# Cluster assignment of the later head pairs: centroids held still while the tokens move

## The chip, the cores and the metric

The kernel runs on one core of one Trainium2 chip. The metric is the device time of one execution in microseconds (us). Five engines work side by side, each through its own list of instructions in order: TensorE (PE; its weight loads are listed apart as PEld), VectorE (DVE), ScalarE (ACT), GpSimd (POOL) and SyncE (SP), which here issues the DMAs.

## The reference, cut to what matters

Attention in which a query sees only the keys of its own cluster, and two wide layers behind it:

```python
# q, k, v: (2, 8, 768, 64); centroids: (8, 16, 64)
q_assign = np.argmax(np.einsum('bhsd,hcd->bhsc', q_n, c_n), axis=-1)   # rows normalised
k_assign = np.argmax(np.einsum('bhsd,hcd->bhsc', k_n, c_n), axis=-1)
mask = q_assign[:, :, :, None] == k_assign[:, :, None, :]
scores = np.where(mask, scale * np.matmul(q, k.transpose(0, 1, 3, 2)), -1e9)
attn = softmax(scores);  x = np.matmul(attn, v)      # -> (1536, 512)
h = x @ w_in;  x = (h * np.cos(h)) @ w_out           # 512 -> 2048 -> 512
h = x @ w2_in; x = elu(h) @ w2_out
```

The change is in the two `einsum` products with the 16 centroids of each head.

## The kernel before

There are 16 heads (2 batches of 8), taken in 8 pairs of 768 tokens, that is 6 blocks of 128. Each head and block of queries is a step, 96 steps in all, 12 to a pair. A step multiplies q with k (`qk`), takes the row maximum on DVE, the exponential on ACT (`P`), turns P on TensorE (`turn`, 6 transposes), and splits what was turned into a high part on ACT (`p_hi`, tile PH) and a low part on DVE (`p_lo`, tile PL), so that TensorE's products with v (`av`, tile px) keep the precision. All fp32 products of the kernel are made of such pairs, hi and lo.

Beside the 12 steps of one pair stands the preparation of the next. `raw_pe` turns k and q on TensorE (tile pt_raw), `raw_out` and `raw_copy` bring them to SBUF on ACT, `raw_low` makes the low part on POOL (one of the four on DVE), and `stack` issues 6 DMAs for each of k and q that lay hi and lo of one head above each other in tiles X0, X1 (and hi alone in T0, T1). `sims_pe` multiplies each of the 24 blocks of a pair (k and q, 2 heads, 6 blocks): the block of the stack is the stationary operand, and the 32 columns of `CC` (16 centroids high, 16 low) move. `sims_add` on DVE adds the high and the low half (2 instructions a pair). Then `sims_scale`, `sims_max`, `sims_eq`, `sims_first`, `best` and `assign` find the cluster, `mask_pe` turns it, `mask_out` writes it, and DMAs lay it under the T tiles, where the next pair's `qk` reads it. The first pair has its own code, one head at a time (`first_pe` and so on), and keeps `sims_pe`.

Seven PSUM buffers matter here: two for the scores of `qk` (tile s), so that `qk` of a step waits for the exponential of two steps before; one for px; and three (`pt_tile`), taken in turn by `turn`, `raw_pe`, the similarities and the mask.

The order on each engine is written by hand in tables: `FIRST`, `PAIR`, `STEP`, `HALF`, `UNIT`, `LAST`, `MLP`, `WINO`, `WB` give each part a time in units of a step, the parts are sorted by it and recorded in that order, and each engine works through its own share in order. `OWN` and tables like `RAW_ON` say on which engine a part runs. After step 96 come the two wide layers (lines 222, 281 and 481 are their products).

Of the kernel before, what the change touches and what calls it, by code (L numbers as in the profile page):

```python
# [61 lines left out]
SSQ = 'quarter'  # L62
XOUT = {0: 'pool', 1: 'pool'}
# [1252 lines left out]
```

## Time and profile before

| | |
|---|---|
| time, median of 3 runs | 780.28 us (776.9 to 780.54) |
| the profiled execution's own time | 778.07 us |
| its span from first to last instruction | 776.3 us |
| PE, DVE, ACT, POOL busy in the span | 98%, 81%, 71%, 50% |
| PE's granted clock | 1.00 |
| head, until the first `qk` (line 1034) starts | 18.61 us |
| attention, until the last `turn` (line 1057) ends | 264.07 us |
| both wide layers and the output | the rest |

The profiled execution is 2.2 us under the median of the three and 1.2 us over the fastest. Busy time is the union of what an engine's records cover; the matmul records overlap each other (one of 128x384 has 340 to 370 ns, and the next starts after about 177), so the pace of PE is read from the chain of work, in which each instruction counts from the end of the one before. The chain names, at every moment, the work that the end of the program waited for. Line numbers are those of the kernel before.

### The profile page before, as it was taken

Reading aid. Unit: us, or ns where it says so; the run is one execution under the profiler, and the core shown is the slowest. Engines: PE = TensorE matmul, PEld = TensorE weight load, DVE = VectorE, ACT = ScalarE, POOL = GpSimd, SP = SyncE. Lnnn points to the kernel's source line nnn. Section 1 sums busy time; section 2 is a strip of 40 time slices with the busy share of each in tenths; the row PEclk is TensorE's granted clock in tenths of the full one; section 3 lists DMA queues with packets and bytes.
Section 4 is the critical chain, followed back from the end, with each engine's and each line's share of the span. In section 5 each row is a group of like instructions: output and inputs, shape, how many; then the busy total and the mean of one; then the engine's idle time right before and its main releaser. Section 6 shows DMA issues by size and latency. Waiting matters only on the chain.

```text
span 776.3 us, 13062 instructions
## 1 busy us (share of the span) xinstructions
PE 761.6 (98%) x4579; PEld 682.2 (88%) x4579; DVE 631.8 (81%) x1026; ACT 548.0 (71%) x1030; POOL 387.0 (50%) x453
## 2 busy tenths in 40 slices
PE   6999999999999999999999999999999999999998
PEld 5899999999898888888999999988888999999996
DVE  7989899899899999997999844699997687754442
ACT  5898998988989978867666755668645554554343
POOL 5676676766866634354555522205236456632221
PEclk9999999999999999999999999999999999999999
DMA  4646647648447295011113168564001222233221
GB/s 104 143 115 148 159 102 163 142 91 197 109 105 264 44 379 194 1 42 73 70 62 123 55 231 291 198 225 155 1 1 41 95 82 82 82 104 115 82 82 54
DMA packets 72145, 93.27 MB, mean 120 GB/s; under 512 B 31440, under 2 KB 52432, under 8 KB 72080
## 3 DMA queue, kind: packets, MB, share of 16 engines
q1 hardware_dynamic: 72080, 92.44, 39.7%
q8 instruction: 36, 0.59, 0.3%
q14 instruction: 29, 0.24, 0.1%
HBM read 58.75 MB, written 15.78 MB: 96 GB/s over the span
## 4 chain that ended last, share of the span: by engine, by line
PE 86%; DVE 6%; ACT 4%; DMA 2%; issue 1%; SPq 0%; POOL 0%; ACTq 0%; DVEq 0%
PE a L281 32%; PE h L481 20%; PE h L222 11%; PE pt L1057 6%; PE px L1088 6%; PE s L1034 3%; PE s L1037 3%; PE pt_sim L869 2%; DVE m L1042 2%; DVE PL L1077 1%; DMA X1k<-lo 1%; PE pt_raw L728 1%; ACT PH L1071 1%; DMA X1q<-lo 1%; ACT P L1048 1%
## 5 line engine op out<-in xcount | busy, mean ns | idle before, releaser
L545 POOL TENSOR_TENSOR GL<-A,GH 128x512 fp32r<-128x512 f32 x60 | 81.1, 1357 | 150.5 <-ACT GH L94 118.6
L281 PE MATMUL a<-GH,slot 128*128 128x512 f32 x384 | 122.9, 390 | 0.0
L281 PE MATMUL a<-slot,GH 128*128 128x512 f32 x384 | 118.5, 389 | 0.0
L1077 DVE TENSOR_TENSOR PL<-pt,PH 128x384 fp32r<-128x384 f32 x192 | 98.3, 548 | 18.1 <-ACT PH L1071 16.9
L1071 ACT ACTIVATE PH<-pt 128x384 fp32r<-128x384 f32 x192 | 84.3, 495 | 15.3 <-PE pt L1057 15.1
L1042 DVE TENSOR_REDUCE m<-s 128x1 f32<-128x768 f32 x96 | 90.8, 946 | 2.1 <-PE s L1037 1.9
L1048 ACT ACTIVATE P<-s,m 128x768 f32<-128x768 f32 x96 | 87.1, 907 | 0.3
L281 PEld LDWEIGHTS a<-GH,slot 128*128 128x128 f32 x384 | 72.2, 188 | 14.6
L1057 PE MATMUL pt<-ident,P 128*128 128x128 f32 x576 | 83.0, 277 | 0.7 <-DVE PL L1077 0.7
L222 PE MATMUL h<-XH,slot 128*128 128x512 f32 x256 | 83.0, 390 | 0.0
L281 PEld LDWEIGHTS a<-slot,GH 128*128 128x128 f32 x384 | 70.9, 188 | 13.7
L481 PE MATMUL h<-XH,slot 128*128 128x256 f32 x384 | 79.2, 281 | 0.0
L281 PE MATMUL a<-GL,slot 128*128 128x512 f32 x192 | 75.0, 390 | 0.0
L281 PE MATMUL a<-slot,GL 128*128 128x512 f32 x192 | 74.7, 389 | 0.0
L1057 PEld LDWEIGHTS pt<-ident,P 128*128 128x128 f32 x576 | 66.6, 140 | 7.4 <-DVE PL L1077 2.2
L392 POOL TENSOR_TENSOR X<-slot 128x512 f32<-128x512 f32 x32 | 50.1, 1578 | 39.8 <-DVE sums L435 34.9
L481 PEld LDWEIGHTS h<-XH,slot 128*128 128x128 f32 x384 | 63.9, 189 | 0.1
L503 DVE TENSOR_TENSOR X<-X 128x256 f32<-128x256 f32 x32 | 24.7, 772 | 46.8 <-ACT X L501 46.8
L94 ACT ACTIVATE GH<-A 128x512 fp32r<-128x512 f32 x85 | 53.2, 625 | 10.1 <-DVE A L253 4.3
L501 ACT ACTIVATE X<-h 128x512 f32<-128x512 f32 x32 | 19.1, 597 | 54.2 <-PE h L481 54.0
L222 PEld LDWEIGHTS h<-XH,slot 128*128 128x128 f32 x256 | 48.0, 188 | 10.0
L1088 PE MATMUL px<-PL,V 128*128 128x384 f32 x192 | 56.2, 368 | 0.0
(198 smaller groups left out, 2007.0 us busy)
## 6 DMA issues: line engine op xcount, KB each, us to landing
raw<-in_moe_w_in_dram SPq DMA_DIRECT2D x32, 512.0 KB, 6.4
raw<-in_moe_w_out_dram SPq DMA_DIRECT2D x32, 512.0 KB, 7.3
sd<-sums SPq DMA_DIRECT2D x32, 384.0 KB, 2.3
sums<-sd SPq DMA_DIRECT2D x32, 384.0 KB, 3.5
nat_k<-in_k_dram SPq DMA_DIRECT2D x16, 192.0 KB, 4.8
nat_q<-in_q_dram SPq DMA_DIRECT2D x16, 192.0 KB, 4.7
nat_v<-in_v_dram SPq DMA_DIRECT2D x8, 384.0 KB, 4.9
xr<-row SPq DMA_DIRECT2D x32, 96.0 KB, 3.6
```

The source lines that it names most:

```text
L94: nc.scalar.activation(out=out, in_=in_, func=AF.Copy)
L222: nc.tensor.matmul(h, lhsT=a[:, kd, :], rhs=b, start=(kd == 0 and i == 0), stop=(kd == NKD - 1 and i == 2))
L281: nc.tensor.matmul(accs[m, t][e], lhsT=a, rhs=b, start=(f == 0 and i == 0), stop=(f == NF - 1 and i == 2))
L392: eng.tensor_tensor(out=u[:, i].rearrange("p e n -> p (e n)").rearrange("p (k f) -> p k f", k=NKD), in0=f32(ih), in1=f32(il), op=ALU.add)
L481: nc.tensor.matmul(o, lhsT=x[:, k], rhs=piece(y, k), start=(k == 0 and n == 0), stop=(k == 1 and n == 2))
L545: eng.tensor_tensor(out=GL, in0=A, in1=f32(GH), op=ALU.subtract)
L1042: nc.vector.tensor_reduce(out=m, in_=st[n]["s"][:, :, 0:HW], axis=AX.XY, op=ALU.max, negate=True)
L1048: nc.scalar.activation(out=P, in_=st[n]["s"][:, :, 0:HW], func=AF.Exp, bias=st[n]["m"], accum_out=den_all[:, u % NDEN, j, r, 0:1])
L1057: nc.tensor.transpose(pt[:, c * 128:(c + 1) * 128], st[n]["P"][:, e, c * 128:(c + 1) * 128], ident)
L1071: nc.scalar.activation(out=ph, in_=pt, func=AF.Copy)
L1077: nc.vector.tensor_tensor(out=pl, in0=pt, in1=f32(ph), op=ALU.subtract)
L1088: nc.tensor.matmul(tx[g][:, 0:HW], lhsT=V2s[pp][:, j, c, :], rhs=halves[g][a][:, c, :], start=(n == 0), stop=(n == 2 * C - 1))
```

## The change

For pairs 2 to 8, `sims_pe` and `sims_add` are replaced by four parts for each half (384 tokens) of the pair.

`pair_cen` (once, on POOL) lays the centroids of each pair on a block diagonal: tile `CCD` has 128 rows (64 dimensions of head 0, 64 of head 1) and, of its 128 columns, those of the wanted tensor filled. `pair_sims` holds CCD still and moves 384 tokens of `hi` and `lo` of q and of k, 4 matmuls that add up in one PSUM tile: k's into 64 rows, q's into 128. It reads `hi` and `lo` themselves, not the stacks that the DMAs make. `pair_keep` copies the result to SBUF (ACT, `KEEP_ON`), `pair_back` turns it back with 3 transposes, and `pair_add` (DVE) adds the high and the low columns. What follows works on the same numbers in another layout. All order tables are remade, `HI2_ON` moves one copy of the first pair from POOL to ACT, and 41 of the 152 entries of `OWN` change engine.

```diff
-PAIR = {'raw_pe:k:0': -2.1142, 'raw_out:k:0': -1.1899, 'raw_low:k:0': 0.3012, ...
+PAIR = {'raw_pe:k:0': -1.2162, 'raw_out:k:0': -1.1229, 'raw_low:k:0': 2.1627, ...
...
+KEEP_ON = {0: "act", 1: "act"}
...
-HI2_ON = {('k', 0): 'act', ('k', 1): 'pool', ('q', 0): 'act', ('q', 1): 'act'}
+HI2_ON = {('k', 0): 'act', ('k', 1): 'act', ('q', 0): 'act', ('q', 1): 'act'}
...
+        CCD = pre.tile([128, NP, 8 * NCL], F32R, name="CCD")
+        turned, backs = {}, {}
+        def pair_cen():
+            need(("cc",))
+            nc.gpsimd.memset(f32(CCD), 0.0)
+            c4 = CC.rearrange("p (a j) n -> p a j n", j=2)
+            for j in range(2):
+                rows = slice(64 * j, 64 * j + 64)
+                copy_on("pool", CCD[rows, :, (4 + 2 * j) * NCL:(6 + 2 * j) * NCL], f32(c4[rows, :, j]))
+            made("ccd")
+        def pair_sims(pp, e):
+            need(("ccd",), *[(x, pp, w, e) for x in ("hi", "lo") for w in "kq"])
+            pt = turned[pp, e] = pt_tile("pt_sim")
+            for w, i in (("q", 0), ("k", 0), ("k", 1), ("q", 1)):
+                n = 128 if w == "q" else 64
+                nc.tensor.matmul(pt[0:n, 0:HW], lhsT=CCD[:, pp % NP, 128 - n:128], rhs=hls[w][i][:, half_slice(e)],
+                                 start=(w == "q" and i == 0), stop=(w == "q" and i == 1))
+            made("pair_sims", pp, e)
+        def pair_keep(pp, e):
+            need(("pair_sims", pp, e))
+            pt = turned[pp, e]
+            turned[pp, e] = pre.tile([128, HW], F32, tag="turned", bufs=2, name="turned")
+            copy_on(KEEP_ON[e], turned[pp, e], pt[:, 0:HW])
+            made("pair_keep", pp, e)
+        def pair_back(pp, e):
+            need(("pair_keep", pp, e))
+            pt = backs[pp, e] = pt_tile("pt_back")
+            for c in range(C // 2):
+                cs = slice(c * 128, (c + 1) * 128)
+                nc.tensor.transpose(pt[:, cs], turned[pp, e][:, cs], ident)
+            made("pair_back", pp, e)
+        def pair_add(pp, e):
+            need(("pair_back", pp, e))
...
+            nc.vector.tensor_reduce(
+                out=sims[pp][:, e * HC:(e + 1) * HC].rearrange("p c b n -> p (c b) n"),
+                in_=backs[pp, e][:, 0:HW].rearrange("p (b t n) -> p b n t", t=2, n=NCL), axis=AX.X, op=ALU.add)
+            made("pair_add", pp, e)
```

TensorE's list in the preparation of the fifth pair, before: half of k's similarities, single ones between the steps' work (L1057 `turn`, L1088 `av`, L1034 and L1037 `qk`); q's 12 stand in one stretch three steps on.

```order
L1088 MATMUL px<-PH,V_1164 128x384 x2
L1057 MATMUL pt<-ident,P 128x128 x3
L869 MATMUL pt_sim<-CC,X0k 128x32
L1057 MATMUL pt<-ident,P 128x128 x3
L1088 MATMUL px<-PL,V_1164 128x384 x3
L869 MATMUL pt_sim<-CC,X1k 128x32
L869 MATMUL pt_sim<-CC,X0k 128x32
L869 MATMUL pt_sim<-CC,X1k 128x32
L1034 MATMUL s<-X0k,X0q 128x384 x2
```

The same place in the changed kernel (L893 `pair_sims`, L909 `pair_back`, L1106 `turn`, L1137 `av`, L1083 and L1086 `qk`), from the second half's `pair_sims` on.

```order
L893 MATMUL pt_sim<-hi,CCD 128x384
L893 MATMUL pt_sim<-hi,CCD 64x384
L893 MATMUL pt_sim<-lo,CCD 64x384
L893 MATMUL pt_sim<-lo,CCD 128x384
L1083 MATMUL s<-X0k,X0q 128x384 x2
L1086 MATMUL s<-T0k,T0q 128x384 x2
L1106 MATMUL pt<-ident,P 128x128 x3
L909 MATMUL pt_back<-ident,turned 128x128 x3
L1106 MATMUL pt<-ident,P 128x128 x3
L1137 MATMUL px<-PH,V_1649 128x384 x3
L1137 MATMUL px<-PL,V_1649 128x384 x3
L909 MATMUL pt_back<-ident,turned 128x128 x3
```

24 matmuls that move 32 columns are gone; 8 that move 384 and 6 transposes stand in fewer places, and one `qk` and three transposes stand between a `pair_sims` and the `pair_back` that waits for its copy.

ScalarE's list at the same place, before (L1048 exponential, L1071 PH, L1130 and L1141 what leaves px, L737 and L743 hi and raw):

```order
L743 ACTIVATE raw<-pt_raw 128x384
L737 ACTIVATE hi<-pt_raw 128x384
L1048 ACTIVATE P,den<-s,m 128x768
L1071 ACTIVATE PH<-pt 128x3x128 x2
L1048 ACTIVATE P,den<-s,m 128x768
L1071 ACTIVATE PH<-pt 128x3x128 x2
L1130 ACTIVATE xr<-px 64x384
L1141 ACTIVATE X<-px 64x384
L1048 ACTIVATE P,den<-s,m 128x768
```

And in the changed kernel (L95 is `pair_keep`; L738, L744, L1097, L1120, L1179, L1190 are the six lines above):

```order
L738 ACTIVATE hi<-pt_raw 128x384
L744 ACTIVATE raw<-pt_raw 128x384
L1097 ACTIVATE P,den<-s,m 128x768
L1120 ACTIVATE PH<-pt 128x3x128 x2
L1097 ACTIVATE P,den<-s,m 128x768
L95 ACTIVATE turned<-pt_sim 128x384
L1120 ACTIVATE PH<-pt 128x3x128 x2
L1179 ACTIVATE xr<-px 64x384
L95 ACTIVATE turned<-pt_sim 128x384
L1190 ACTIVATE X<-px 64x384
L1097 ACTIVATE P,den<-s,m 128x768
```

The two copies stand between two exponentials, where none stood.

## Rows read from the trace of the kernel before

**Rows 1.** The page: busy time by engine, and the chain's shares by engine.
```profile
PE 761.6 (98%) x4579; PEld 682.2 (88%) x4579; DVE 631.8 (81%) x1026; ACT 548.0 (71%) x1030; POOL 387.0 (50%) x453
...
PE 86%; DVE 6%; ACT 4%; DMA 2%; issue 1%; SPq 0%; POOL 0%; ACTq 0%; DVEq 0%
```

**Rows 2.** Windows: length, busy us by engine, clock, DMA; pairs, transition, wide layer.
```profile
96.37:126.63 30.26, 30.23 (x213) 28.32 (x212) 27.50 (x55) 27.88 (x65) 21.34 (x33) 1.00 0.60 137
126.63:157.57 30.94, 30.43 (x214) 28.36 (x212) 28.19 (x56) 28.02 (x65) 21.32 (x33) 1.00 0.65 142
...
187.82:218.67 30.85, 30.27 (x213) 28.29 (x212) 27.64 (x55) 27.99 (x65) 21.33 (x33) 1.00 0.61 144
...
226.00:258.00 32.00, 30.45 (x200) 28.51 (x199) 30.26 (x56) 31.59 (x69) 21.96 (x20) 1.00 0.55 183
...
300.00:350.00 50.00, 50.00 (x245) 42.35 (x244) 47.79 (x67) 36.99 (x56) 21.69 (x17) 1.00 0.06 25
```

**Rows 3.** Chain of waits in time order, 113 to 128 us: start, us, what.
```profile
113.44 0.53 PE px L1088 x3
...
114.30 0.35 PE s L1034 x2
...
116.68 0.33 PE pt_raw L728 x3
...
118.70 0.81 PE pt L1057 x6
...
119.86 0.45 PE s L1034 x2
...
123.29 0.66 PE pt L1057 x6
...
126.63 1.14 PE pt_sim L869 x11
```

**Rows 4.** Timeline of PE: similarities that waited for a DMA; in brackets idle, releaser.
```profile
27.35 0.36 PE L869 MATMUL pt_sim<-CC,X1k 128*128 128x32 f32 x2 [0.54 <-DMA X1k<-lo]
...
156.92 0.25 PE L869 MATMUL pt_sim<-CC,X1q 128*128 128x32 f32 x1 [0.43 <-DMA X1q<-lo]
...
210.43 0.37 PE L869 MATMUL pt_sim<-CC,X1k 128*128 128x32 f32 x2 [0.51 <-DMA X1k<-lo]
```

**Rows 5.** Groups of instructions: busy us, mean ns, then idle before.
```profile
L743 ACT ACTIVATE raw<-pt_raw 128x384 f32<-128x384 f32 x21 | 10.4, 496 | 0.2
...
L876 DVE TENSOR_REDUCE sm<-pt_sim 128x192 f32<-128x384 f32 x14 | 7.7, 552 | 0.1
```

**Rows 6.** Timeline of ACT in the same pair.
```profile
104.64 0.86 ACT L1071 ACTIVATE PH<-pt 128x384 fp32r<-128x384 f32 x2
105.38 0.92 ACT L1048 ACTIVATE P<-s,m 128x768 f32<-128x768 f32 x1
...
118.42 0.94 ACT L1048 ACTIVATE P<-s,m 128x768 f32<-128x768 f32 x1
119.21 0.25 ACT L1048 ACTIVATION_READ_ACCUMULATOR P<-s,m 128x1 f32 x1
...
121.36 0.91 ACT L1071 ACTIVATE PH<-pt 128x384 fp32r<-128x384 f32 x2 [0.26 <-PE pt L1057]
```

**Rows 7.** Timeline of POOL: the last low part of the same pair.
```profile
118.65 1.00 POOL L752 TENSOR_TENSOR lo<-raw,hi 128x384 fp32r<-128x384 f32 x1 [0.42 <-ACT hi L737]
```

**Rows 8.** Chain of waits in the head.
```profile
16.81 0.36 DVE sm L876
17.17 0.28 DVE M L935
...
17.50 0.52 PE pt_mask L944 x3
```

**Rows 9.** Timeline of POOL in the head: first square and low part of pair 2.
```profile
18.02 1.47 POOL L828 TENSOR_TENSOR sq<-nat_k 128x768 f32<-128x768 f32 x1 [0.22 <-issue]
...
21.23 1.00 POOL L752 TENSOR_TENSOR lo<-raw,hi 128x384 fp32r<-128x384 f32 x1
```

More of the change, by code (lines that the diff above doesn't have):

```diff
@@ new lines @@
+PAIR = {'raw_pe:k:0': -1.2162, 'raw_out:k:0': -1.1229, 'raw_low:k:0': 2.1627, 'raw_pe:k:1': -0.5582, 'raw_out:k:1': -0.3666, 'raw_low:k:1': 0.0171, 'stack:k': 3.2351, 'raw_pe:q:0': 1.144, 'raw_out:q:0': 1.3604, 'raw_low:q:0': 2.2027, 'raw_pe:q:1': 1.644, 'raw_out:q:1': 2.0896, 'raw_low:q:1': 2.6137, 'stack:q': 3.2967, 'square:k': -0.448, 'square:q': -1.0107, 'sum_sq:k': 1.6306, 'sum_sq:q': 1.1242, 'seed': 2.2387, 'norms': 4.9678, 'sims_scale': 6.3541, 'sims_max': 6.3759, 'sims_first': 6.6512, 'load_nat:k': -7.1463, 'load_nat:q': -7.2335, 'load_nat:v': 3.0434, 'raw_copy:k:0': -0.8153, 'raw_copy:k:1': -0.0355, 'raw_copy:q:0': 1.2556, 'raw_copy:q:1': 2.276, 'best': 7.3105, 'sims_eq': 6.5858, 'values_hi:0': 7.8287, 'values_lo:0': 7.9611, 'values_hi:1': 8.019, 'values_lo:1': 9.0409, 'norm_step:0': 2.8631, 'norm_step:1': 3.0606, 'norm_step:2': 3.4295, 'norm_step:3': 3.6274, 'assign': 7.8532, 'mask_pe': 8.4304, 'mask_out': 8.6084, 'pair_sims:0': 3.9595, 'pair_sims:1': 3.043, 'pair_keep:0': 4.3053, 'pair_keep:1': 3.5714, 'pair_back:0': 4.5395, 'pair_back:1': 5.207, 'pair_add:0': 4.8399, 'pair_add:1': 5.6206}
@@ L871, in sims_pe @@
                 made("sim", pp, w, n)
+        CCD = pre.tile([128, NP, 8 * NCL], F32R, name="CCD")
[31 more added lines that the diff above has]
+            need(("pair_back", pp, e))
+            if pp not in sims:
+                sims[pp] = pre.tile([128, C, 4, NCL], F32, tag="sm", bufs=1, name="sm")
+            nc.vector.tensor_reduce(
+                out=sims[pp][:, e * HC:(e + 1) * HC].rearrange("p c b n -> p (c b) n"),
+                in_=backs[pp, e][:, 0:HW].rearrange("p (b t n) -> p b n t", t=2, n=NCL), axis=AX.X, op=ALU.add)
+            made("pair_add", pp, e)
         def sims_add(pp, w, js):
@@ L882, in sims_of @@
         def sims_of(pp, js):
-            return sims[pp][:, :, js[0]] if len(js) == 1 else sims[pp].rearrange("p w h c n -> p w (h c) n")
+            return sims[pp][:, :, js[0]] if len(js) == 1 else sims[pp]
         def sims_scale(pp, js):
-            need(("norm", (pp, js)), ("sims", pp, "k", js), ("sims", pp, "q", js))
+            need(("norm", (pp, js)), *([("pair_add", pp, e) for e in range(2)] if pp else [("sims", pp, w, js) for w in "kq"]))
             sm = sims_of(pp, js)
+            r = nrm[pp].rearrange("p w h c -> p c (w h)") if pp else of_heads(nrm[pp], js)
             eng = nc.vector if pp == 0 else nc.gpsimd
-            eng.tensor_tensor(out=sm, in0=sm, in1=of_heads(nrm[pp], js).unsqueeze(3).to_broadcast(list(sm.shape)),
+            eng.tensor_tensor(out=sm, in0=sm, in1=r.unsqueeze(3).to_broadcast(list(sm.shape)),
                               op=ALU.mult)
@@ L919, in best @@
             if pp not in bests:
-                bests[pp] = pre.tile([128, 2, 2, C], F32, tag="best", bufs=1, name="best")
-            nc.vector.tensor_reduce(out=of_heads(bests[pp], js), in_=sims_of(pp, js), axis=AX.X, op=ALU.max)
+                bests[pp] = pre.tile([128, C, 4] if pp else [128, 2, 2, C], F32, tag="best", bufs=1, name="best")
+            nc.vector.tensor_reduce(out=bests[pp] if pp else of_heads(bests[pp], js), in_=sims_of(pp, js), axis=AX.X, op=ALU.max)
             made("best", pp, js)
@@ L931, in assign @@
             else:
-                sh = [128, 4, C, NCL]
-                m = M.rearrange("p c b n -> p b c n")[:, :, :, 0:NCL]
-                be = bests[pp].rearrange("p w h c -> p (w h) c")
+                sh = [128, C, 4, NCL]
+                m = M[:, :, :, 0:NCL]
+                be = bests[pp]
             nc.vector.tensor_tensor(out=m, in0=desc.unsqueeze(1).unsqueeze(1).to_broadcast(sh),
@@ L1213 @@
                         at(t0, fn, pp, *own)
-                elif fn in (raw_pe, raw_out, raw_copy, raw_low, stack, values_hi, values_lo):
+                elif fn in (raw_pe, raw_out, raw_copy, raw_low, stack, values_hi, values_lo, pair_sims, pair_keep, pair_back,
+                            pair_add):
                     at(t0, fn, pp, *own)
```

21 lines of the change are left out of this document (10 added, 11 removed).

## The prediction

> **What bounds the kernel now.** I read the page first, then windows of busy time over single pairs, then the chain of waits inside one pair, and last the timelines of ScalarE and GpSimd there. The page gives TensorE 98% and puts 86% of the chain on it [rows 1]. Busy time alone proves little, since matmul records overlap. In a clean pair of 30.26 us TensorE has 30.23, ScalarE 27.88, VectorE 27.50 and GpSimd 21.34 us [rows 2]; the chain of that pair runs through TensorE's instructions one behind the other at a steady pace, six transposes in 0.66 us, three products with 384 moving columns in 0.53, eleven similarities in 1.14 [rows 3]. So there the pace of TensorE is the time, and work taken from it is time saved, as long as ScalarE, which idles only 30.26 - 27.88 = 2.38 us a pair, keeps up. Two of the pairs are longer by 0.68 and 0.59 us [rows 2], each holding a similarity that waited for a DMA of the stacks, and a third such wait of 0.54 us stands in the head [rows 4]. Between 226 and 258 us ScalarE is full instead (31.59 of 32.00) [rows 2]. In the wide layers TensorE has 50.00 of 50.00 us, so nothing is to be had there.
>
> **What goes from TensorE, per pair (7 pairs).** 24 similarities at 1.14 / 11 = 0.104 us are 2.49. They also delay what follows: the scores behind a run of them take 0.45 for two matmuls in place of 0.35, three times in this pair, and the six transposes behind four of them 0.81 in place of 0.66 [rows 3]: 0.45 more. Together 2.94 us.
>
> **What comes to it.** 8 products with 384 moving columns at 0.53 / 3 = 0.177 are 1.41; 6 transposes at 0.33 / 3 = 0.110 (as the raw ones) are 0.66 [rows 3]; 2.07 together. Gain 0.87 a pair, 6.1 us in seven. The trace shows no product with this block diagonal, so I bound it: at the dearest rows, 0.45 / 2 = 0.225 and 0.81 / 6 = 0.135, the new work is 2.61, and with no delays credited to the old the pair loses 0.12; at the cheapest, 0.35 / 2, it gains 0.88. I take 0.87, since the products of px have the same shape in stationary and moving operand. 7 pairs: +0.8 to -6.2, taken -6.1.
>
> The 32 columns that a similarity moves do not explain 0.104 us, which the row shows. [...]
>
> **What comes to the others.** ScalarE gets 2 copies of 128x384 a pair, 496 ns each as the copy `raw` [rows 5], 0.99 of busy time; where it works without a break the next starts 0.37 us later (two PH start at 104.64 and what follows them at 105.38, half of 0.74 each [rows 6]), so 0.74 of its pace. VectorE's two sums keep their input, 128x384, and their 552 ns [rows 5]: nothing. GpSimd gets a memset and two small copies once.
>
> **The new waits.** The scores of a step wait for the exponential of two steps before (two buffers). In this pair ScalarE has no idle from 104.64 to 121.36 us, through the whole raw stage [rows 6]. At its end an exponential ends at 119.21 + 0.25 = 119.46, and TensorE's next scores start at 119.86 [rows 3]: 0.40 us to spare. The two copies stand just there, ahead of the next exponential, and push it by 0.74: a wait of 0.34. Behind the waiting scores TensorE holds the transposes and the products with v, so this is paid in full. The wait of `pair_sims` itself seems covered: the last low part ends at 119.65 [rows 7], 2.64 us after its raw transposes (117.01 [rows 3]), and in the new order TensorE has 6 products, a step's scores, 6 transposes and 3 products between, 1.06 + 0.70 + 0.66 + 0.53 = 2.95. If that cover is gone, low parts cost what they are late. `pair_back` has scores and three transposes (1.03) to cover a copy of 0.50. I count 0.35 a pair, 2.5 us; the bounds are 0 (ScalarE's 2.38 us take it up) and 0.99 a pair, 6.9.
>
> **The DMA waits.** `pair_sims` reads hi and lo, so the stacks are needed only by the next pair's scores, some steps later. 0.68 + 0.59 + 0.54 = 1.8 us go [rows 2, 4]; at least 1.0, if a low part is late where the DMA was.
>
> **The head.** The first mask waits for an `assign` that stands behind a sum of the last similarities (0.36, at 16.81) though it does not need it [rows 8]. In the new order it stands ahead of that sum: -0.4. Against it, GpSimd now has both squares of the second pair ahead of the three low parts: one square with its sums takes 21.23 - 18.02 = 3.2 us [rows 9], so the low parts end near 18.0 + 6.4 + 3.0 = 27.4, where the old similarities began at 27.35 [rows 4]. I leave that at nothing; bounds -1 and +1 for the head.
>
> **The rest.** From 226 to 258 us ScalarE's work stays as it is, so 0; bounds -1.5 and +1.5 (TensorE's 32.00 - 30.45) [rows 2]. In the wide layers the remade order can only lose: +0.5, one gap such as those of rows 4; bounds 0 and +3.
>
> **The sum.** -6.1 + 2.5 - 1.8 - 0.4 + 0 + 0.5 = -5.3 against the profiled execution's 778.07, so 772.8. That execution is 2.2 us under the median of the three and 1.2 over the fastest; the mean of the four is 778.95, 0.9 higher. On that level the forecast is 773.6.
>
> **Rivals.**
>
> *ScalarE takes back what TensorE gives.* If the copies cost their whole 0.99 a pair at the place above, the pair changes by 0.99 - 0.87 = +0.12. With the DMA waits gone the sum is 0.8 - 1.8 - 0.4 + 0.5 = -0.9: 778.0. For it: ScalarE's long stretch without idle. Against it: 2.38 us of idle in the same pair, and shorter use of the three PSUM buffers (the old similarities of k hold one from 2.2 to 4.3 in `PAIR`, about two steps).
>
> *Slower: ScalarE becomes the bound of every pair.* The place is the raw stage. If TensorE already follows ScalarE there, through the two score buffers, then what it saves is worth nothing and each pair grows by the copies, 7 x 0.99 = 6.9; `pair_sims` then waits for hi and lo that ScalarE brings later, so the DMA waits are only exchanged. 6.9 - 0.4 + 0.5 = +7.0: 786. It decides from the point where the copies exceed the idle that ScalarE can reach in order: 0.99 against the 0.40 us above, if the 2.38 us lie elsewhere for good. Against it: the chain of the pair is TensorE's alone [rows 3]. The Trainium skill's page Trainium Kernel Development and Optimization (section "Best Practices") speaks for this side: tiling speeds up compute "but not PSUM evacuation", and the change buys TensorE's time with two more evacuations; no run here shows yet which of the two ends last.
>
> *More gained.* No new wait, and the transition gains 1.0: -5.3 - 2.5 - 1.0 = -8.8, 770.1.
>
> **How the numbers follow.** Forecast 0.55 (its own range 770 to 777), ScalarE takes it back 0.23, slower 0.13, more gained 0.09. The range 769.5 to 781 leaves out the slower case and a little below. A measurement of this kernel can tell about 0.5% from no change, 3.9 us, so faster means under 776.4 and slower over 784.2: faster holds the forecast but for its upper end, the case of more gained and a little of the second, 0.57; slower 0.13; between 0.30.
>
> **What would show it.** Clean pairs of 29.5 to 30.0 us in the windows, TensorE still full in them; no wait of TensorE for a DMA between 20 and 220 us; scores (L1034's successor) waiting for an exponential, some 0.3 us a pair; ScalarE at 28.9 us a pair. Pairs of 30.3 and longer with ScalarE without idle would make the forecast wrong, as would gaps of TensorE in the wide layers of more than 1 us, or `pair_sims` waiting for GpSimd in each pair.

## The result, and the profile after

The changed kernel takes 783.85 us (median of 7 runs, 782.89 to 784.69) where the kernel before takes 780.03 (7 runs, 776.9 to 781.38): ratio 1.0058, 95% interval 1.0038 to 1.0078. It is slower by 0.6%, and the time lies 10 us above the forecast of 773.6 and 2.8 above the upper end of the range. The profiled execution took 784.19, with a span of 782.3 (776.3 before). Lines 52 to 872 have moved by 1 (L222 is now L223), those from 890 to 1213 by 49 (L1034 is L1083).

Four points that both traces show, by the start of the same instruction, split the 6.0 us between the two spans (the medians are 3.8 apart):

| | before | after | change |
|---|---|---|---|
| raw transposes of q (pt_raw), third pair | 53.22 | 54.03 | head +0.81 |
| the same, eighth pair | 205.25 | 204.91 | five periods 152.03, 150.88: -1.15 |
| first product of the next token block, h<-XH (L481, L482) | 342.87 | 347.82 | stretch 137.62, 142.91: +5.29 |
| end of the span | 776.3 | 782.3 | 433.4, 434.5: +1.05 |

The head's part is known only to about 1 us: four other traces below with the same code up to there (e1, e3, e5, e11) pass the first point at 53.71, 53.66, 54.58 and 54.61, so it lies between +0.4 and +1.4.

The page after (busy by engine, then the chain's shares by engine), and windows of one pair, of two stretches behind attention and of the wide layer (columns as in [rows 2]):

```profile
PE 760.7 (97%) x4509; PEld 678.2 (87%) x4509; DVE 613.6 (78%) x1030; ACT 559.2 (71%) x1051; POOL 379.9 (49%) x445
...
PE 68%; DVE 10%; DMA 8%; ACT 8%; SPq 2%; issue 2%; POOL 1%; ACTq 0%; POOLq 0%
```
```profile
117.33:147.51 30.18, 29.47 (x202) 27.68 (x201) 27.05 (x53) 28.90 (x67) 21.37 (x34) 1.00 0.61 130
...
280.00:285.00 5.00, 2.10 (x8) 1.38 (x7) 5.00 (x6) 5.00 (x8) 0.00 (x0) 0.93 1.07 374
285.00:290.00 5.00, 5.00 (x18) 3.98 (x17) 3.15 (x5) 2.66 (x4) 0.00 (x0) 0.73 1.06 376
300.00:350.00 50.00, 50.00 (x231) 41.78 (x230) 44.63 (x58) 40.04 (x62) 21.93 (x14) 1.00 0.04 17
```

A pair lasts 30.18 us, 0.08 less than the clean one of [rows 2], with TensorE 29.47 busy instead of 30.23 and ScalarE 28.90 instead of 27.88. TensorE stands still for 2.90 of the 5 us from 280, and in the 5 us behind them the granted clock is 0.73. What TensorE waited for (total, times, longest):

```profile
PE pt L1106 <- ACT hi L738: 3.3, 6, 0.6
PE h L223 <- DVE A L254: 2.9, 1, 2.9
PE pt L1106 <- DVE PL L1126: 2.6, 9, 0.8
...
PE h L482 <- DVE sums L363: 0.8, 1, 0.8
```

The first is six times the same place, one in each of six pairs; TensorE and ScalarE there (start, duration, then in brackets the idle time and who ended it):

```profile
115.06 0.52 PE L1086 MATMUL s<-T0k,T0q 80*128 80x384 f32 x2
116.13 0.88 PE L1106 MATMUL pt<-ident,P 128*128 128x128 f32 x6 [0.55 <-ACT hi L738]
```
```profile
113.78 0.89 ACT L1120 ACTIVATE PH<-pt 128x384 fp32r<-128x384 f32 x2
114.69 0.48 ACT L1179 ACTIVATE xr<-px 64x384 f32<-64x384 f32 x1
115.20 0.49 ACT L744 ACTIVATE raw<-pt_raw 128x384 f32<-128x384 f32 x1
115.59 0.48 ACT L738 ACTIVATE hi<-pt_raw 128x384 fp32r<-128x384 f32 x1
```

`turn` needs a PSUM buffer that pt_raw holds until `hi` has read it, and `hi` stands behind xr and raw on ScalarE. The new work itself, in the same pair:

```profile
120.12 0.51 PE L893 MATMUL pt_sim<-hi,CCD 128*128 128x384 f32 x2
120.47 0.52 PE L893 MATMUL pt_sim<-lo,CCD 128*64 128x384 f32 x2
...
124.46 0.49 PE L909 MATMUL pt_back<-ident,turned 128*128 128x128 f32 x3
```

Two products in 0.35, as forecast (0.177 each). Behind attention, TensorE and VectorE:

```profile
280.26 0.39 PE L282 MATMUL a<-GH,slot 128*128 128x512 f32 x1
283.54 0.50 PE L223 MATMUL h<-XH,slot 128*128 128x512 f32 x1 [2.90 <-DVE A L254]
...
285.23 1.05 PE L223 MATMUL h<-XH,slot 128*128 128x512 f32 x2
...
287.75 0.62 PE L223 MATMUL h<-XH,slot 128*128 128x512 f32 x2
```
```profile
281.07 1.22 DVE L177 TENSOR_TENSOR slot<-u,slot 128x1024 fp32r<-128x1024 f32 x1
282.20 1.28 DVE L254 TENSOR_TENSOR A<-h,R 128x512 f32<-128x512 f32 x2
```

The second A ends at 283.48, and the first product of the fifth F block (a slice of 128 of the 2048 hidden columns) starts at 283.54. From 285.23 to 286.51 three products take 1.28 us, from 287.75 to 288.43 three take 0.68: 3 x 512 columns are 1.28 us at 1.2 GHz and 0.64 at 2.4, the two levels of TensorE's clock.

### The profile page after: what moved, and what is told of

It is laid out like the page before. It is cut to its first block, busy times and chain, and to the rows that moved or that the text cites. A ratio compares the mean times of both kernels' runs of the same rounds, so it can differ in the third digit from the quotient of the medians.

```text
span 782.3 us, 12962 instructions
## 1 busy us (share of the span) xinstructions
PE 760.7 (97%) x4509; PEld 678.2 (87%) x4509; DVE 613.6 (78%) x1030; ACT 559.2 (71%) x1051; POOL 379.9 (49%) x445
## 4 chain that ended last, share of the span: by engine, by line
PE 68%; DVE 10%; DMA 8%; ACT 8%; SPq 2%; issue 2%; POOL 1%; ACTq 0%; POOLq 0%
PE a L282 32%; PE h L482 20%; PE h L223 11%; DMA row<-sum 4%; DVE m L1091 3%; DVE PL L1126 3%; ACT PH L1120 2%; DMA xr<-row 2%; ACT P L1097 2%; PE pt L1106 2%; PE px L1137 2%; DMA nat_q<-in_q_dram 1%; PE pt_sim L893 1%; ACT Z L1016 1%; SPq L609 1%
## 5 line engine op out<-in xcount | busy, mean ns | idle before, releaser
L546 POOL TENSOR_TENSOR GL<-A,GH 128x512 fp32r<-128x512 f32 x60 | 83.8, 1401 | 144.6 <-ACT GH L95 109.4
L1126 DVE TENSOR_TENSOR PL<-pt,PH 128x384 fp32r<-128x384 f32 x192 | 101.0, 547 | 12.7 <-ACT PH L1120 11.0
L1106 PE MATMUL pt<-ident,P 128*128 128x128 f32 x576 | 88.4, 275 | 6.0 <-ACT hi L738 3.3
L1120 ACT ACTIVATE PH<-pt 128x384 fp32r<-128x384 f32 x192 | 85.5, 493 | 5.0 <-PE pt L1106 4.6
L1097 ACT ACTIVATE P<-s,m 128x768 f32<-128x768 f32 x96 | 87.1, 907 | 2.6 <-DVE m L1091 2.0
L223 PE MATMUL h<-XH,slot 128*128 128x512 f32 x256 | 84.3, 395 | 3.0 <-DVE A L254 2.9
L1106 PEld LDWEIGHTS pt<-ident,P 128*128 128x128 f32 x576 | 69.2, 140 | 16.0 <-ACT hi L738 5.2
L482 PE MATMUL h<-XH,slot 128*128 128x256 f32 x384 | 81.7, 282 | 0.0
L95 ACT ACTIVATE GH<-A 128x512 fp32r<-128x512 f32 x88 | 54.9, 626 | 17.5 <-DVE A L541 11.3
L482 PEld LDWEIGHTS h<-XH,slot 128*128 128x128 f32 x384 | 65.0, 190 | 0.7
L393 POOL TENSOR_TENSOR X<-slot 128x512 f32<-128x512 f32 x32 | 48.4, 1523 | 35.2 <-DVE sums L436 31.2
L223 PEld LDWEIGHTS h<-XH,slot 128*128 128x128 f32 x256 | 48.7, 191 | 13.9 <-DVE A L254 3.3
L1137 PE MATMUL px<-PH,V 128*128 128x384 f32 x192 | 58.4, 381 | 0.1
L482 PE MATMUL h<-XL,slot 128*128 128x256 f32 x192 | 54.2, 282 | 0.0
```

The source lines that it names most:

```text
L95: nc.scalar.activation(out=out, in_=in_, func=AF.Copy)
L223: nc.tensor.matmul(h, lhsT=a[:, kd, :], rhs=b, start=(kd == 0 and i == 0), stop=(kd == NKD - 1 and i == 2))
L393: eng.tensor_tensor(out=u[:, i].rearrange("p e n -> p (e n)").rearrange("p (k f) -> p k f", k=NKD), in0=f32(ih), in1=f32(il), op=ALU.add)
L482: nc.tensor.matmul(o, lhsT=x[:, k], rhs=piece(y, k), start=(k == 0 and n == 0), stop=(k == 1 and n == 2))
L546: eng.tensor_tensor(out=GL, in0=A, in1=f32(GH), op=ALU.subtract)
L1097: nc.scalar.activation(out=P, in_=st[n]["s"][:, :, 0:HW], func=AF.Exp, bias=st[n]["m"], accum_out=den_all[:, u % NDEN, j, r, 0:1])
```

## Experiments

The yardstick of the first two groups is the stretch of the table, from the raw q of the eighth pair to the first product of the next token block: 137.62 before, 142.91 after.

### Do the remade tables of the wide layers cost the time?

Theory at first: yes. Rival: the new order of attention starves the change to the wide layers, whatever tables stand there.

```diff
 # e1: changed kernel
-LAST, OWN, MLP, WINO, WB = (changed)
+LAST, OWN, MLP, WINO, WB = (before)
 # e2: kernel before, the same five tables of the changed one
 # e3: changed kernel, LAST and OWN alone of before
```

> The changed kernel with the five tables of the wide layers (LAST, OWN, MLP, WINO, WB) of the kernel before; the similarities, their PAIR, STEP, HALF, UNIT and FIRST tables stay as changed. Theory (the remade transition tables cost the time, not the similarities): the 2.90 us wait of TensorE for VectorE's A at the change to the wide layers goes, the granted clock stays near 1.00 from 280 to 290 us, and the time falls by 5 to 6 us against the changed kernel, to 778.3 (777 to 780.5), that is 1 to 2 us below the kernel before. Rival (the new attention order itself starves the transition, whatever tables stand behind it): the wait stays and the time is 783 to 785.

> The kernel before with the five tables of the wide layers (LAST, OWN, MLP, WINO, WB) of the changed kernel; its similarities are as before. Theory (the remade tables cost the time): slower than before by 5 to 6 us, 785.5 (783.5 to 787), with a wait of TensorE of some 3 us at the change to the wide layers. Rival (the new attention order starves the transition): no loss, 780 (779 to 781).

> The changed kernel with LAST and OWN alone of the kernel before (change to the wide layers), MLP, WINO and WB as changed. Theory: of the 5.9 us lost behind attention about 5.0 are got back here, and the 0.9 at the start of the first Winograd round stay: 779.3 (778 to 781). If the wide layers' own tables (MLP, WINO, WB) carry the loss instead: 783 to 784.

Measured: e1 781.09 (stretch 141.48), e2 783.53 (141.78), e3 782.74 (140.09). In e1 a sum of the wide layer (T1) stands ahead of the scaling of some attention rows, which enter it unscaled; its time alone is read. None of the three has the 2.90 us wait, but e1 and e3 gain 1 to 3 us, not 5 to 6, and TensorE waits earlier; in e3:

```profile
264.61 0.55 PE L1106 MATMUL pt<-ident,P 128*128 128x128 f32 x3 [1.68 <-DVE PL L1126]
```

Each set of tables is fitted to the attention order that it was made with, and mixing costs at the seam either way. So this says nothing clean on which part is to blame; neither theory is confirmed.

### The shared PSUM bank

```diff
 # e4
-KEEP_ON = {0: "act", 1: "act"}
+KEEP_ON = {0: "dve", 1: "dve"}
```

> The changed kernel with the two copies of the similarities per pair (turned) on VectorE in place of ScalarE. Theory (TensorE's new wait of 0.55 us per pair comes from ScalarE running late with hi and raw): ScalarE falls from 28.9 to about 27.9 us a pair, the wait of turn on hi shrinks to 0.1 to 0.3, the pairs get 0.2 to 0.4 us shorter and the whole 1.5 to 3 us: 781.8 (780.5 to 783). Rival (the wait is a matter of the written order alone, or VectorE with 28 us of 30.2 becomes late): pairs unchanged or longer, 783.5 to 786.

779.50 (779.16 to 780.38), 4.35 us under the changed kernel, far more than expected, but not where it was expected: the pairs keep their 30.17 us and the six waits for `hi` (3.3 us); the 2.90 us wait is gone, the stretch is 138.13. TensorE's order is the same in both. What differs is where the tile allocation puts h of the third and the fourth F block, which take over two of the three buffers of `pt_tile` (banks 4 to 6; the first two h take those of the scores). These are handed out in the order in which they come free, and which engine frees one shifts the rotation. In the changed kernel h of the fourth F block lies in bank 4, before in 5. The next pool's first h, that of the fifth block, takes bank 4 in every kernel here, and so has to wait until the last reader of the old tile, A of the fourth block, is done. By the allocation of each built kernel the bank does not follow the amount of work that moves: with none of the 14 copies on VectorE h of the fourth block lies in bank 4, with one (e5) in 5, with twelve (e6) in 4, with all (e4) in 5. That gives a test.

```diff
 # e5: one copy moved; e6: in its place "act" if pp == 7 else "dve", six pairs moved
-            copy_on(KEEP_ON[e], turned[pp, e], pt[:, 0:HW])
+            copy_on("dve" if (pp, e) == (7, 0) else "act", turned[pp, e], pt[:, 0:HW])
 # e11: changed kernel, third and fourth F block change places on TensorE
-'g1': (1.1555, -0.4134, 5.0263, 4.546)
+'g1': (1.1555, -0.4134, 4.546, 5.0263)
 # e9: kernel before, RAW_ON['k', 0] of the eighth pair alone 'dve'
```

> The changed kernel with one single copy (turned, eighth pair, first half) on VectorE, all the others on ScalarE. Each kernel says by its tile allocation in which PSUM bank the four early products h of the wide layer lie: in the changed kernel h of the fourth F block lies in bank 4, the bank that the first h of the next pool takes, so that the fifth block's first product waits until VectorE's A of the fourth has read it; with one copy moved the buffers of attention rotate otherwise and h lies in bank 5. Theory (the loss at the change to the wide layer is this shared bank, not ScalarE's load): the 2.90 us wait goes, the clock stays at 1.00 from 285 to 290, the pairs stay as they are, 779.5 (778.5 to 780.5). Rival (ScalarE's load over all pairs makes the transition late): one copy of 0.5 us changes nothing, 783 to 784.5.

> All copies (turned) on VectorE but the two of the eighth pair, which stay on ScalarE. By the allocation h of the fourth F block lies in bank 4 again. Theory (shared bank): the wait of about 2.9 us at 283 us is back and the time is that of the changed kernel, 783.8 (782.5 to 785), though ScalarE is as light as in the run with all copies on VectorE. Rival (ScalarE's load decides): 779.5 to 780.5, as with all copies on VectorE.

> The changed kernel with its bank as it is, but the third and the fourth F block change places on TensorE, so that h of the third block lies in bank 4; VectorE's order is unchanged and reads the third block's h first, 0.64 us ahead of the fourth's. Theory (the first product of the fifth block waits for exactly that reader): the wait of h for A falls from 2.90 to about 2.3 us, and the time by about that and a little of the lower clock, 783.0 (782 to 783.8). Rival (the wait is for something else, a weight slot or a DMA): 2.9 us and 783.8 as before.

> The kernel before, with one copy less: the first half of k of the eighth pair alone is split by VectorE out of PSUM (lo) in place of ScalarE's copy and GpSimd's difference. By the allocation h of the fourth F block then lies in bank 4, as in the changed kernel. Theory (the bank costs only where its last reader is late; in the old order of the change to the wide layer VectorE has read h of the fourth block before TensorE comes): no wait of h for A, the time of the kernel before, 779.5 (778.5 to 780.5). Rival (the shared bank costs by itself): a wait of 2 to 3 us at 280 us and 783 to 784.5.

One copy of 0.5 us moved in one pair is enough: e5 779.50, stretch 138.14. The place of the wait, the two A on VectorE, and the clock behind them:

```profile
280.85 0.39 PE L282 MATMUL a<-GH,slot 128*128 128x512 f32 x1
281.07 0.39 PE L223 MATMUL h<-XH,slot 128*128 128x512 f32 x1
```
```profile
282.78 1.28 DVE L254 TENSOR_TENSOR A<-h,R 128x512 f32<-128x512 f32 x2
```
```profile
285.00:290.00 5.00, 5.00 (x24) 4.15 (x23) 4.96 (x8) 4.24 (x7) 0.00 (x0) 1.00 1.07 376
```

VectorE is no earlier for it: its second A ends at 284.06 (283.48 in the changed kernel), but TensorE has begun the fifth block at 281.07 and waits for nothing. So it was not the late A alone that held it.

e6 is back at 784.32, stretch 142.82, with ScalarE's load as light as in e4 (28.16 us a pair):

```profile
283.44 0.79 PE L223 MATMUL h<-XH,slot 128*128 128x512 f32 x1 [2.85 <-DVE A L254]
```
```profile
117.33:147.51 30.18, 29.47 (x202) 27.65 (x201) 27.74 (x55) 28.16 (x66) 21.40 (x34) 1.00 0.58 133
280.00:285.00 5.00, 2.15 (x7) 1.44 (x6) 5.00 (x6) 5.00 (x8) 0.00 (x0) 0.82 1.07 378
285.00:290.00 5.00, 5.00 (x20) 4.02 (x19) 3.29 (x6) 2.79 (x4) 0.00 (x0) 0.84 1.07 374
```

In e11 the reader is the first A of the two, and the wait is 0.66 us shorter, about one A (0.64); time 783.24, stretch 140.70:

```profile
283.59 0.50 PE L223 MATMUL h<-XH,slot 128*128 128x512 f32 x1 [2.24 <-DVE A L254]
```
```profile
282.85 1.28 DVE L254 TENSOR_TENSOR A<-h,R 128x512 f32<-128x512 f32 x2
```

And e9, the kernel before with h of the fourth block put into bank 4: 779.18, against 777.99 for the kernel before, measured beside it (ratio 1.0016, 0.9999 to 1.0033), with no wait, since in the old order A of that block comes early:

```profile
278.29 0.68 DVE L254 TENSOR_TENSOR A<-h,R 128x512 f32<-128x512 f32 x1
```
```profile
280.12 0.39 PE L223 MATMUL h<-XH,slot 128*128 128x512 f32 x1
```

So it takes both: the bank, which the new attention order happens to leave to the fourth block, and the remade LAST, which puts that block's A behind the third's and behind the preparing of weights on VectorE (both A from 282.20, where e9 has the fourth's alone at 278.29). e1 and e3 agree: with the older LAST, and h of the fourth block in bank 4 by their allocation, neither has the wait. Together the two cost 142.91 - 138.14 = 4.8 us by the traces (2.9 of wait, the rest mostly the lower clock) and 4.35 by the medians.

### What sets the time of a pair?

Without the bank the kernel only equals the one before. First the longest wait was taken away: the raw transposes of q one product earlier, raw and hi ahead of xr, with all copies on VectorE (e7) or one (e8). In e12 (on e10, below) VectorE takes ScalarE's raw of this half.

```diff
-'raw_pe:q:0': 1.144, 'raw_copy:q:0': 1.2556, 'raw_out:q:0': 1.3604
+'raw_pe:q:0': 0.9, 'raw_copy:q:0': 1.1, 'raw_out:q:0': 1.13
 # e12
-RAW_ON['q', 0] = 'act'; 'raw_low:q:0': 2.2027
+RAW_ON['q', 0] = 'dve'; 'raw_low:q:0': 1.15
```

> All copies on VectorE, and of each pair's first raw half of q the three transposes (pt_raw) stand one product earlier on TensorE and their two copies (raw, hi) ahead of xr on ScalarE. Theory (the pairs lose 0.55 us each because turn waits for the PSUM buffer that pt_raw holds until hi): the wait of turn on hi falls from 0.55 to 0 to 0.15 in each of six pairs, the period of a pair from 30.16 to 29.6 to 29.8 us, and the time from 779.5 to 776.5 (775.5 to 778). Rival (the wait only moves: ScalarE or VectorE or the exponential is late next): the period stays at 30.1 and the time at 779 to 780.

> As the run before it (raw q early, raw and hi ahead of xr), but with one copy alone on VectorE and the others on ScalarE, so that ScalarE keeps its 28.9 us a pair. Theory (the order, not the load, made the wait): the same period of 29.6 to 29.8 us and 776.7 (775.5 to 778). Rival (ScalarE with 28.9 us in 29.7 is too full): the wait comes back in another place, 778 to 780.

> As the run with raw q early and the mask early, and ScalarE's copy raw of the first half of q goes for every pair: VectorE takes the low part from PSUM (lo, 0.56 us), as it does for the second half of k. Two copies turned (seventh and eighth pair, first half) are on VectorE, so that the early h lie in banks 5 and 6. In the run before, TensorE's products px behind the raw transposes start 0.05 us after ScalarE's X (116.07 and 116.12 us), so ScalarE in the raw stage still sets the pace there. Theory (ScalarE's order in the raw stage, not its load over the pair, is the bound): X and the exponential come 0.4 to 0.5 us earlier, the period of a pair falls from 30.07 to 29.6 to 29.9 us, and the time from 778.3 to 776.5 (775.5 to 777.6). Rival (the transposes now wait for VectorE's lo, which holds the PSUM buffer longer than hi did): the period stays at 30.0 to 30.2 and the time at 778 to 779.

e7 778.83, e8 778.89: the wait fell to 0.5 and 0.2 us in all, but the period only from 30.18 to 30.05 and 30.04. In e8, TensorE and ScalarE at the same place:

```profile
115.10 0.88 PE L1106 MATMUL pt<-ident,P 128*128 128x128 f32 x6
...
116.10 0.79 PE L1137 MATMUL px<-PH,V 128*128 128x384 f32 x3
```
```profile
114.56 0.48 ACT L738 ACTIVATE hi<-pt_raw 128x384 fp32r<-128x384 f32 x1
...
115.56 0.48 ACT L1190 ACTIVATE X<-px 64x384 f32<-64x384 f32 x1
```

`turn` still starts 0.06 us behind hi (115.04), and px 0.06 behind X (116.04), which frees the only px buffer: the wait has moved, in pieces too short for the list. e12 came out above its range: 780.70, period 30.18, and a wait of 1.0 us more in the head, where `pt_sim` waits for GpSimd. ScalarE's load makes no difference here (e7 and e8 have 28.3 and 28.9 us of it a pair). That left the premise of the forecast, that TensorE's pace is the time. Four runs test it with TensorE's work alone:

```diff
 # e13 (on e10), e15 (on before): 12 products px fewer a pair; e14, e16: the same 12 twice
+            if a == 1 and c >= 3: return        # in av
 # e17: e13 and all copies on VectorE; e18: e13 and the edit of e12
```

The texts of these runs count 6 products and 1.06 us a pair, half of what was changed. Three of the six go in each half of the attention, and a pair has four such halves: 12 products, 12 x 0.177 = 2.12 us a pair and 17 us in all. The page of e15 has 96 matmuls fewer than that of the kernel before (x4579 in [rows 1]):

```profile
PE 755.7 (98%) x4483; PEld 664.8 (86%) x4483; DVE 628.8 (81%) x1026; ACT 548.0 (71%) x1030; POOL 386.8 (50%) x453
```

So the periods that go by TensorE's pace have to be read as 28.0 (e13), 32.2 (e14), 28.1 (e15) and 32.4 (e16).

> As the run with raw q and the mask early (778.3), and of every half of the attention three of the six products of the low parts with v (px from PL, c 3 to 5) are left out, so the output lacks a part of the low-order sum; all other instructions stay. TensorE has 6 products of 0.177 less a pair, 1.06 us, and 48 less in all, 8.5 us. Theory (in the new order a pair is set by a loop over ScalarE and the buffers, TensorE has room in it): the period falls from 30.07 to 29.6 to 29.9 only, time 774 to 777. Rival (TensorE's pace sets the pair as it did): 29.0 and 769.8 (769 to 771).

> The same kernel with these 6 products a pair done twice (the low-order sum is counted double in part). Theory (room in the loop): the pauses take up a part, the period rises from 30.07 by 0.3 to 0.8, time 781 to 785. Rival (TensorE's pace): by the full 1.06, to 31.1, time 786.8 (786 to 788).

> The kernel before with the same 6 products a pair left out. If TensorE's pace set the old pairs, as the prediction had it: the clean period falls from 30.26 to 29.2 and the time by 8.5, to 770.5 (769.5 to 772). If a loop set them already: the period falls to 29.7 to 30.1 only, time 775 to 778.

> The kernel before with the 6 products a pair done twice. If TensorE's pace set the old pairs: 31.3 a pair and 787.5 (786.5 to 788.5). If not: 30.6 to 31.0, time 782 to 786.

| | period of a pair | time |
|---|---|---|
| before; 2.12 us less (e15); 2.12 more (e16) | 30.26; 29.96; 31.78 | 779.08; 779.53; 791.45 |
| e10; less (e13); more (e14) | 30.07; 29.97; 31.02 | 778.33; 776.08; 785.63 |

(Clean pairs; two of e15's five periods are longer, 30.80 and 30.21. Its profiled execution took 776.0, its runs spread from 775.98 to 783.44.) One pair of e13, then of e15:

```profile
113.18:143.15 29.97, 28.69 (x190) 25.20 (x188) 27.11 (x54) 28.75 (x68) 21.47 (x33) 1.00 0.65 145
```
```profile
113.43:143.39 29.96, 29.50 (x200) 26.16 (x199) 27.22 (x55) 27.89 (x66) 21.34 (x34) 1.00 0.60 140
```

Of 2.12 us added to TensorE a pair of the kernel before pays 1.52 and one of the new order 0.95; of 2.12 taken away they give back 0.30 and 0.10, and the time of e15 is not told apart from that of the kernel before (ratio 1.0003, 0.9980 to 1.0025). So both orders have room in TensorE. An estimate of it: if an added product costs the 0.177 of [rows 3], TensorE's own work is at most 31.78 - 2.12 = 29.66 us a pair before and 31.02 - 2.12 = 28.90 in e10, which is 0.6 and 1.2 under the periods. Both stop at the same 29.96. e15 also shows what a full TensorE in [rows 2] was worth: with 2.12 us less to do it is still listed as 29.50 busy of 29.96.

> As the run of the new order with 6 products px a pair left out (period 29.97, 776.1), and all copies turned on VectorE: ScalarE has 2 copies less a pair, 0.74 us, outside the raw stage. If ScalarE's load over the pair holds the period: 29.3 to 29.6 and 772 to 774. If its stretch in the raw stage holds it: the period stays within 0.1 of 29.97, 775.5 to 776.7.

> As the run of the new order with 6 products px a pair left out, and ScalarE's copy raw of the first half of q left to VectorE (lo from PSUM): ScalarE has 0.4 us less in its gapless stretch of the raw stage. If that stretch holds the period: 29.5 to 29.7, and 773 to 776 (the head is 1.2 us longer in this order). If ScalarE is not what holds it: 29.9 to 30.1, 777 to 778.5.

e17 775.86, period 29.87; e18 776.71, 29.82: ScalarE's 0.74 us outside the raw stage bring 0.10, 0.4 us within it 0.15. So neither ScalarE's load nor that stretch is the floor. What TensorE waits for in e13, in the five periods together:

```profile
PE pt L1106 <- DVE PL L1126: 3.9, 5, 0.8
PE pt L1106 <- ACT hi L738: 1.6, 5, 0.3
```

The longer of the two is for VectorE's PL, which no run tried to bring earlier. That the floor is a loop of several engines through the few PSUM buffers is a guess; what the floor at about 29.9 consists of stays open.

### The head

```diff
 # e10: e8, and
-'mask_pe:1': -5.8236, 'mask_out:k:1': -5.316
+'mask_pe:1': -7.3, 'mask_out:k:1': -7.2
```

> As the run with raw q early and one copy on VectorE, and the second mask of the first pair (mask_pe, T0k) due at -7.3 and -7.2 in place of -5.8 and -5.3, so that VectorE writes T0k ahead of the product of the similarities with the norms (1.47 us). Theory (TensorE's wait of 0.57 to 0.87 us for T0k at 20 us comes from that order): the wait goes, the head is 0.5 to 0.9 us shorter and the time 778.2 (777.2 to 779). Rival (the shortened head is taken back at a later gate): the wait goes and the time stays at 778.9.

The wait of 0.87 at 20 us (e8) is gone, since T0k now stands ahead of two other instructions on VectorE:

```profile
20.06 0.69 PE L1086 MATMUL s<-T0k,T0q 80*128 80x384 f32 x1 [0.87 <-DVE T0k L1009]
```
```profile
17.68 0.55 DVE L1009 TENSOR_SCALAR T0k<-pt_mask 16x384 fp32r<-16x384 bf16 x1 [0.39 <-PE pt_mask L993]
```

The raw q of the second pair starts 0.9 us earlier (21.56 instead of 22.46), but the third pair at 53.44, as in e8 (53.50). By that the gain is taken back before 53 us, as the rival has it; yet this point varies by about 1 us between traces of the same code (see the first table), and e10's median is 0.56 lower, though measured apart from e8's, so it stays open. e10 takes 778.33 (778.21 to 778.61): 5.5 us better than the changed kernel, and not told apart from the kernel before (777.99 beside it; ratio 0.9988, 0.9974 to 1.0002). It is the best whole version found, and not shown to beat both.

## Why the prediction was wrong

The terms as the prediction put them, laid on the four parts of the first table (0.52 is its gain of 0.87 less 0.35 a pair), and what the runs give:

| term | forecast | measured |
|---|---|---|
| TensorE's work per pair | -0.87 | -0.86 |
| new waits per pair | +0.35 | +0.62, less the DMA wait that went |
| DMA waits | gone, -1.8 | gone |
| head with one pair and a DMA wait | -0.4 - 0.52 - 0.54 = -1.5 | +0.81 |
| five periods with a DMA wait | -2.6 - 0.68 = -3.3 | -1.15 |
| stretch: one pair, a DMA wait, transition | -0.52 - 0.59 + 0 = -1.1 | +5.29 |
| the rest of the wide layers | +0.5 | +1.05 |

- *The work* came out at its price, in part by luck. From the start of each instruction to that of the next, without listed waits and as means of the five periods, the similarities took 2.68 us a pair and now take 1.40, and 0.57 for the turning back: 0.71 less. The other 0.15 is what is left of shifts elsewhere: px takes 0.43 more, other parts less. TensorE in all went from 30.32 to 29.46.
- *The step that failed in the pairs* is "the pace of TensorE is the time, and work taken from it is time saved". The full busy time and the chain through TensorE [rows 2, 3] were read as proof. They were none: of 2.12 us of TensorE's work taken away, the kernel before gives back 0.30 a pair (e15), and of 2.12 added it pays 1.52 (e16). It stood 0.30 us above a second limit, and 0.87 us less for TensorE could not bring 0.87.
- *The new waits* came where the rival "ScalarE becomes the bound" put them, in the raw stage (0.55 for hi and 0.16 for PL, against 0.09 a pair for a DMA before), not at the scores behind the copies, where the forecast did. But the price of that rival was wrong too: pairs did not grow by the copies, and without them on ScalarE they last 30.17 (e4). That the time came out near its 786 is chance, for its 6.9 us were to come from the pairs, which got shorter. For this rival the prediction had cited the Trainium skill, Trainium Kernel Development and Optimization (section "Best Practices"): tiling speeds up compute "but not PSUM evacuation". Here it matters little which engine evacuates: with the two copies on VectorE a pair is 0.10 us shorter (e13 against e17).
- *The DMA waits*: right; none is listed for TensorE after the first load.
- *The head*: the mask did start earlier (16.97 instead of 17.50), but T0k came behind another instruction on VectorE (0.57), and X0k cost 1.10 instead of 0.61. Whether repairing T0k alone brings anything is open (e10).
- *The step that decided the sign* is "the remade order can only lose: +0.5, one gap such as those of rows 4". It missed by 6.4 us in the stretch, more than all the other parts. It was one gap, but of 2.90 us, with a lower clock behind it. The gap's size is seen in no row of before: it hangs on which bank the rotation leaves to which tile. The prediction read the order of the instructions, not the allocation. It did name gaps over 1 us in the wide layers as what would make it wrong. The further +1.05 belongs to the remade tables of the wide layers: with the old five (e1) this part takes 433.44, as before (433.42). It holds the 0.8 us wait for `sums` at the second token block, which e1 does not have; e8 and e10, which come to that block 0.8 to 1 us earlier than the kernel before, pass the place at 430.6 and 430.8, as it does (430.65), so what they had gained ends there.
- Without the shared bank the parts nearly cancel. In e5's trace they are head +1.4, periods -1.1, stretch +0.5 and the rest +1.05, so 1.8 us over the profiled execution of before; by the times e5 is level with it, ratio 1.0005 (0.9994 to 1.0016).

## What to carry to other kernels

An engine that is busy throughout and holds the chain may still have room: leave out a little of its work, count in the trace how much went, and see whether the time follows, before pricing a saving. Where tiles of a new stage take over PSUM banks from a pool that hands them out as they come free, look up in the allocation which bank each first tile gets and who reads it last, for any change of the earlier stage can shift it. Order tables are fitted to each other, so exchanging some of them tells little about which is to blame.

## What the runs showed of the hardware

- After an idle time of 2.90 us TensorE's granted clock was 0.66 from 283 to 288 us, after 2.85 us (e6) 0.66 as well, after 2.24 us (e11) 1.00 throughout. The 0.73 and 0.84 of the windows from 285 differ only by how much of the slow time lies ahead of 285. Against e5, with no such wait, the stretch is 4.8, 4.7 and 2.6 us longer, so 1.9, 1.8 and 0.3 more than the wait itself. The changed kernel, then e6:

```profile
283.00:288.00 5.00, 4.46 (x13) 3.51 (x14) 4.05 (x5) 2.83 (x4) 0.00 (x0) 0.66 1.08 377
```
```profile
283.00:288.00 5.00, 4.56 (x14) 3.63 (x15) 3.95 (x5) 2.79 (x5) 0.00 (x0) 0.66 1.07 378
```

- In e2 the clock was low once more in the head (0.86 from 30 to 60 us), and the third pair started at 57.37 instead of 53.22. The column for 0 to 30 us tells nothing of the first matmuls: the kernel before has 1.00 there, but its first two products s take 0.88 us, where two take 0.35 in [rows 3].

```profile
18.61 0.99 PE L1034 MATMUL s<-X0k,X0q 128*128 128x384 f32 x2
19.49 1.01 PE L1037 MATMUL s<-T0k,T0q 80*128 80x384 f32 x2
```
